# Sliding-window attention into a gated MLP on one core: batch 0's first eight groups lose their normalising pass, and the opening's list is put in another order

## The chip, the cores and the metric

The kernel runs on one core of one Trainium2 chip. The time is device microseconds (us) of one execution. The median of the runs before the change is 303.38 us (three runs, 303.17 to 303.96). The core has five engines that run side by side, each through its own instructions in order: TensorE (PE, matmuls; its weight loads are PEld), VectorE (DVE), ScalarE (ACT), GpSimd (POOL, which here also issues most loads) and SyncE (SP, which issues DMAs only). They wait for each other through semaphores. SBUF is the working memory, PSUM the memory that TensorE writes.

## What is computed

q, k and v are 8 batches x 8 heads x 576 positions x 64, in float32. A position attends to itself and the 63 before it:

```python
scores = (q @ k.T) / 8
mask = (rel >= 0) & (rel < 64)            # rel = pos_query - pos_key
scores = np.where(mask, scores, -1e9)
attn = np.exp(scores - scores.max(-1))
attn = attn / (attn.sum(-1) + 1e-9)
x = (attn @ v)                            # -> 4608 tokens x 512 (8 heads x 64)
h = x @ w_in                              # 512 x 2048
out = (h * np.cos(h)) @ w_out             # 2048 x 512 -> 4608 x 512, float32
```

## The kernel before

**Tiling.** The 4608 tokens are nine blocks of 512 (`mt`). Attention is worked in units of 64 queries by 128 keys (its own 64 keys and the 64 before). Two heads form a pair and share a unit: one head on partitions 0 to 63, the other on 64 to 127. A *group* is four units, so one 128x512 tile. The first eight groups (`n < n_first`) are batch 0: pair p, g = 0 for tokens 0 to 255 and g = 1 for tokens 256 to 511. The other groups are those of the later batches and of batch 0's last 64 tokens. Groups 8 to 18 are listed by hand too.

**One group, before.** `g_scores` (L296) writes the mask into PSUM by a matmul with the identity (L307) and adds the scores (L314). `g_max` (L320) takes the negated row maximum on DVE (L324). `g_exp` (L335) makes four exponentials on ACT, 128x128 each, with the row sum as a second result (L341, which the profile shows as ACTIVATE and ACTIVATION_READ_ACCUMULATOR). `g_inv` (L345) takes the reciprocal of the 128x4 sums on DVE (L351). `g_norm` (L354) multiplies the 128x512 exponentials by it, on POOL for the first eight groups (L358), and makes bfloat16 weights. `g_trans` (L367) transposes them on PE (L374), or by a DMA on SP's queue (L377) for groups not in `direct`; `g_put` (L380) copies the transposed weights to SBUF (through `copy`, L124). Every line 124 in the profile is that helper.

**Values and the first block.** `values_half(a, g)` (L405) multiplies the weights of pairs 2a and 2a+1 with v, for 256 tokens (L411); `put_x_half` (L415) copies the product to `xT` (L418, by L124). Block 0 goes in halves of 256 tokens: `first_half(g, f)` (L420) makes eight matmuls of 128x256 (L425) into one of five PSUM banks, `sine_half` (L429) takes the sine on ACT (L431), `gate_half` (L433) multiplies on DVE (L437) and frees the bank. A half of the block needs `xT` of both values of a. `second_part` (L439) is the second product (L444). Block 1 and later use lines 461, 692, 695 and 709.

**What sets the order.** The opening, up to the start of block 1, is one hand-written string, `FIRST` (L46 to L64). Each word is a step, recorded in that order on all engines: `Lq`, `Lk`, `Lv`, `Lwi`, `Lwo` are loads (POOL's queue, except pair 0's q and k of batch 0 by SP); `tq`/`tk` transposes and `pq`/`pk` their copies (capitals are batch 1); `s m e i n w c` the steps of a group named pair.g; `v` and `x` the values and their copy, named a.g; `h S g` first product, sine and gate, named half.f; `o` the second product; `zA zB zC` spread batch 0's v by 64 partitions; `tb` and `tb2` load ACT's tables; `G` words are groups 8 to 18. An engine thus does its share of the words from left to right. Each load of POOL's queue waits for the landing of the one eight before it. After the list, each block calls `pump`, which issues planned steps by their due times (`at`).

The small PSUM tiles with the tag "t" (transposes, values) come from a pool of three; the tiles "s" and "e" in SBUF from six.

Of the kernel before, what the change touches and what calls it, by code (L numbers as in the profile page):

```python
# [10 lines left out]
def _safe_warn(msg, *a, **kw):  # L11
# [3 lines left out]
F32 = mybir.dt.float32  # L15
BF16 = mybir.dt.bfloat16
AF = mybir.ActivationFunctionType
ALU = mybir.AluOpType
# [7 lines left out]
GF = 4  # L26
# [7 lines left out]
T = 2 * Q  # L34
LAGS = (0.2, 1, 3, 3.2, 3.8)
SKEW = 3
DIRECT = (0, 7, 8)
OUTS = 3
FILL = (6, 12)
TURNED = {4: 2, 5: 2, 6: 2, 7: 6}  # L40
# [3 lines left out]


FIRST = (  # L46
# [18 lines left out]
)  # L65


# [1 line left out]
def kernel(  # L69
# [9 lines left out]
    nc = tc.nc  # L79
    B, H, S, D = q.shape  # L80
    assert (B, H, S, D) == (8, 8, 576, 64)
    scale = 1.0 / math.sqrt(D)
# [8 lines left out]
    const = ctx.enter_context(tc.tile_pool(name="const", bufs=1))  # L91
    ld = ctx.enter_context(tc.tile_pool(name="ld", bufs=2))
    att = ctx.enter_context(tc.tile_pool(name="att", bufs=3))
    moe = ctx.enter_context(tc.tile_pool(name="moe", bufs=2))
    ps = ctx.enter_context(tc.tile_pool(name="ps", bufs=1, space=PSUM))
    ps_t = ctx.enter_context(tc.tile_pool(name="ps_t", bufs=3, space=PSUM))
# [9 lines left out]
    mask16 = const.tile([128, 6, 128], BF16, name="mask16")  # L106

    small = const.tile([128, 1], F32, name="small")
    w_sums = const.tile([128, 2, n_ff // 2, MT // 2], BF16, name="w_sums")

    st = {}
# [6 lines left out]
    half = MT // 2  # L118
# [4 lines left out]
    def copy(engine, out, in_):  # L123
        {"a": nc.scalar.copy, "p": nc.gpsimd.tensor_copy}.get(engine, nc.vector.tensor_copy)(out, in_)  # L124
# [126 lines left out]
    n_first = len(groups)  # L251
# [18 lines left out]
    last = n_listed + 4, n_listed + 5  # L270
    direct = set(range(n_first)) | {n_first + i for i in DIRECT} | set(last)

# [61 lines left out]

    def g_exp(n):  # L335
        s, negm = st.pop(("s", n)), st.pop(("m", n))
        e = att.tile([128, GF, 128], F32, tag="e", name="e", bufs=6)
        den = att.tile([128, GF], F32, tag="den", name="den", bufs=8)
        for u, (_, _, j, *_) in enumerate(groups[n]):
            c = slice(0, 128 if j or n < n_first else 64)  # L340
            nc.scalar.activation(e[:, u, c], s[:, u, c], AF.Exp, bias=negm[:, u:u + 1], scale=1.0 if n < n_first else -1.0,  # L341
                                 accum_out=den[:, u:u + 1])
        st["e", n] = e, den

    def g_inv(n):  # L345
        e, den = st["e", n]
        for u, (_, _, j, *_) in enumerate(groups[n]):
            if j == 0 and n >= n_first:
                nc.vector.memset(e[:, u, 64:128], 0.0)
        rden = att.tile([128, GF], F32, tag="rden", name="rden", bufs=8)  # L350
        nc.vector.reciprocal(out=rden[:, 0:len(groups[n])], in_=den[:, 0:len(groups[n])])  # L351
        st["r", n] = rden

    def g_norm(n, engine="p"):  # L354
        (e, _), rden = st.pop(("e", n)), st.pop(("r", n))
        w = att.tile([128, GF, 128], BF16, tag="w", name="w", bufs=8)
        u = len(groups[n])
        (nc.gpsimd if engine == "p" else nc.vector).tensor_tensor(out=w[:, 0:u], in0=e[:, 0:u], op=ALU.mult,  # L358
                                in1=rden[:, 0:u].unsqueeze(2).to_broadcast([128, u, 128]))
        st["w", n] = w  # L360

    def put_wT(n, wT):
        for i, (b, p, j, *h) in enumerate(groups[n]):
            for e in range(2):
                st["wT", (b, 2 * p + e, j, h[0]) if h else (b, p, j, e)] = wT[:, i, 64 * e:64 * e + 64]

    def g_trans(n):  # L367
        w, u = st.pop(("w", n)), len(groups[n])
        if n in direct:
            st["tw", n] = t_ps = ps_t.tile([128, GF, 128], BF16, tag="t", name="tw_ps")  # L370
            for i in range(GF if n == FILL[0] else 0):
                nc.tensor.transpose(t_ps[:, i], ident, ident)
            for i in range(u):
                nc.tensor.transpose(t_ps[:, i], w[:, i], ident)  # L374
            return
        wT = att.tile([128, GF, 128], BF16, tag="wT", name="wT", bufs=20)
        nc.sync.dma_start(out=wT[:, 0:u], in_=w[:, 0:u].rearrange("p u c -> p (u c)"), transpose=True)  # L377
        put_wT(n, wT)

    def g_put(n, engine=None):  # L380
        wT, u = att.tile([128, GF, 128], BF16, tag="wT", name="wT", bufs=20), len(groups[n])
        copy(engine, wT[:, 0:u], st.pop(("tw", n))[:, 0:u])
        put_wT(n, wT)


# [26 lines left out]
                                     lhsT=vtiles[0][:, max(j - 1, 0), 128 * (2 * a + p) + 64 * h:128 * (2 * a + p) + 64 * h + 64],  # L412
                                     rhs=st["wT", (0, 2 * a + p, j, h)], start=True, stop=True, skip_group_check=True)

    def put_x_half(a, g, engine=None):  # L415
        if ("xT", 0) not in st:
            st["xT", 0] = att.tile([128, PAIRS, MT], BF16, tag="xT", name="xT", bufs=2)
        copy(engine, st["xT", 0][:, 2 * a:2 * a + 2, half * g:half * g + half], st.pop(("o", a, g)))  # L418

    def first_half(g, f, which):  # L420
        st["h", g, f] = h_ps = bank(BANKS[which], "h_ps")
# [30 lines left out]
    def exp_table():  # L452
        nc.scalar.activation(small, small, AF.Exp, scale=0.0)
# [126 lines left out]
    for i, (b, jobs, banks) in enumerate(bursts):  # L580
        t = T * (b - 1)
# [49 lines left out]
    for n in range(16):  # L631
        i, f = divmod(n, 4)
# [6 lines left out]
        at(T + 4 - 0.1 * i, g_trans, n_listed - i)  # L639

    make_identity(nc, ident)
    nc.vector.memset(small, 0.0)
    exp_table()

    def spread_first(lo, hi):
# [15 lines left out]
             "y": lambda half_, engine: spread_v(1, half_, engine),  # L661
             "s": lambda p, g, which: g_scores(2 * p + g, which), "m": lambda p, g: g_max(2 * p + g),
             "e": lambda p, g: g_exp(2 * p + g), "i": lambda p, g: g_inv(2 * p + g),
             "n": lambda p, g, engine: g_norm(2 * p + g, engine), "w": lambda p, g: g_trans(2 * p + g),
             "c": lambda p, g, engine: g_put(2 * p + g, engine), "v": values_half, "x": put_x_half,
             "tb": sine_table, "tb2": exp_table, "h": first_half, "S": sine_half, "g": gate_half,
             "Gs": g_scores, "Gm": g_max, "Ge": g_exp, "Gi": g_inv, "Gn": g_norm, "Gw": g_trans, "Gc": g_trans,
             "Gp": g_put, "V": lambda p: values(1, p), "X": lambda p, engine: put_x(1, p, engine),
             "o": second_part, "oc": put_out}
    for step in FIRST.split():  # L670
# [5 lines left out]
    for mt in range(1, n_mt):  # L676
# [5 lines left out]
        for ff in range(n_ff):  # L682
# [8 lines left out]
            e = ff % 2  # L691
# [8 lines left out]
        for ms0 in range(0, MT // 128, 2):  # L700
            o_sb = moe.tile([128, 2, d_model], F32, tag="out", name="out_sb", bufs=OUTS)
            o_ps = [bank(which, "out_ps") for which in (("O1",) if mt == n_mt - 1 and ms0 else ("O1", "O0"))]
            for e in range(2):
# [4 lines left out]
                for ff in range(n_ff):  # L708
                    nc.tensor.matmul(out=o_ps[e], lhsT=gT[ff // 2][:, ff % 2, ms * 128:ms * 128 + 128],  # L709
                                     rhs=w_out_sb[:, ff], start=ff == 0, stop=ff == n_ff - 1)  # L710
# [38 lines left out]
```

## Time and profile before

| | |
|---|---|
| median of three runs | 303.38 us (303.17 to 303.96) |
| the profiled execution | 304.26 us, of which the span is 302.5 us |
| granted TensorE clock | 1.00 |
| PE busy | 290.5 us, 96% of the span |
| DVE busy | 233.8 us, 77% |
| ACT busy | 232.2 us, 77% |
| POOL busy | 208.7 us, 69% |
| first product of block 0 starts | 22.20 us after the span's start |
| its second product starts | 38.65 us |
| block 1's first product starts | 58.05 us |

In the profile's rows a line names the engine, the line of the kernel, the operation, the tile written and the tiles read, the shapes, and after "x" how many. A group row gives the busy time in us and the mean ns of one. A row of the timeline begins with the start and the length in us; the bracket is idle time of the engine just before it and what ended that time.

### The profile page before, as it was taken

Reading aid. Unit: us, or ns where it says so; the run is one execution under the profiler, and the core shown is the slowest. Engines: PE = TensorE matmul, PEld = TensorE weight load, DVE = VectorE, ACT = ScalarE, POOL = GpSimd, SP = SyncE. Lnnn points to the kernel's source line nnn. Section 1 sums busy time; section 2 is a strip of 40 time slices with the busy share of each in tenths; the row PEclk is TensorE's granted clock in tenths of the full one; section 3 lists DMA queues with packets and bytes.
Section 4 is the critical chain, followed back from the end, with each engine's and each line's share of the span. In section 5 each row is a group of like instructions: output and inputs, shape, how many; then the busy total and the mean of one; then the engine's idle time right before and its main releaser. Section 6 shows DMA issues by size and latency. Waiting matters only on the chain.

```text
span 302.5 us, 8484 instructions
## 1 busy us (share of the span) xinstructions
PE 290.5 (96%) x2920; PEld 162.4 (54%) x2920; DVE 233.8 (77%) x913; ACT 232.2 (77%) x781; POOL 208.7 (69%) x238
## 2 busy tenths in 40 slices
PE   3889999999999999999999999999999999999995
PEld 2668844554454544545454445444544454785484
DVE  3898877988887886788668875887688658985893
ACT  5898698877987699869986999689978997305610
POOL 7899558996799779987999699878995860000000
PEclk9999999999999999999999999999999999999999
DMA  7999999999999994999999998999599944003013
GB/s 150 180 205 168 196 192 133 102 136 155 237 125 111 219 158 88 98 143 185 198 105 155 164 183 118 136 196 178 110 110 128 198 84 156 0 3 141 1 35 106
DMA packets 158588, 41.47 MB, mean 137 GB/s; under 512 B 146960, under 2 KB 154192, under 8 KB 158544
## 3 DMA queue, kind: packets, MB, share of 16 engines
q0 software_dynamic: 100192, 18.06, 83.8%
q1 hardware_dynamic: 58352, 22.85, 41.5%
q8 instruction: 23, 0.38, 0.5%
q14 instruction: 21, 0.17, 0.2%
HBM read 36.70 MB, written 9.44 MB: 153 GB/s over the span
## 4 chain that ended last, share of the span: by engine, by line
PE 84%; DMA 11%; POOL 3%; DVE 1%; issue 1%; POOLq 0%
PE h_ps L461 37%; PE out_ps L709 28%; PE out_ps L555 8%; DMA w_out<-in_moe_w_out_dram 7%; DMA q<-in_q_dram 4%; PE out_ps L444 3%; PE s_ps L292 3%; PE o_ps L393 3%; POOL w L358 2%; PE tq_ps L206 1%; PE tw_ps L374 0%; DVE xT L124 0%; PE s_ps L314 0%; POOL w_in L191 0%; DVE negm L324 0%
## 5 line engine op out<-in xcount | busy, mean ns | idle before, releaser
L461 PE MATMUL h_ps<-xT,w_in 128*128 128x512 bf16 x512 | 115.1, 379 | 0.2
L695 DVE TENSOR_TENSOR gT<-h_ps,sin 128x512 bf16<-128x512 f32 x128 | 85.1, 688 | 25.8 <-ACT sin L692 25.2
L692 ACT ACTIVATE sin<-h_ps 128x512 f32<-128x512 f32 x128 | 73.8, 598 | 37.0 <-PE h_ps L461 36.7
L341 ACT ACTIVATE e<-s,negm 128x128 f32<-128x128 f32 (+1 forms) x256 | 97.1, 381 | 2.9 <-DVE negm L329 1.9
L709 PE MATMUL out_ps<-w_out,gT 128*128 128x512 bf16 x384 | 85.3, 379 | 0.0
L358 POOL TENSOR_TENSOR w<-e,rden 128x512 bf16<-128x512 f32 (+1 forms) x68 | 69.0, 1031 | 19.3 <-DVE rden L351 14.8
L461 PEld LDWEIGHTS <-w_in 128*128 128x128 bf16 x512 | 49.0, 98 | 54.5
L709 PEld LDWEIGHTS <-gT 128*128 128x128 bf16 x384 | 36.5, 98 | 43.1
L329 DVE CUSTOM_DVE_ANT_0 s<-s_ps,mask 128x128 f32<-128x128 f32 (+1 forms) x256 | 56.0, 277 | 2.5 <-PE s_ps L314 2.2
L341 ACT ACTIVATION_READ_ACCUMULATOR e<-s,negm 128x1 f32 x256 | 47.9, 187 | 0.0
L169 POOL DMA_DIRECT2D q<-in_q_dram x36 | 28.6, 796 | 9.7 <-DMA q<-in_q_dram 3.2
L175 POOL DMA_DIRECT2D v<-in_v_dram x40 | 34.2, 869 | 0.8 <-DMA q<-in_q_dram 0.6
L169 POOL DMA_DIRECT2D k<-in_k_dram x36 | 28.5, 794 | 2.4 <-DVE negm L329 0.9
L351 DVE RECIPROCAL rden<-den 128x4 f32<-128x4 f32 (+1 forms) x73 | 12.1, 166 | 18.3 <-ACT e L341 18.1
L124 POOL COPY v<-v 64x1536 bf16<-64x1536 bf16 (+3 forms) x16 | 22.9, 1431 | 0.4
L329 DVE DVE_READ_ACCUMULATOR2_ANT negm<- 128x1 f32 x256 | 21.3, 83 | 0.0
L124 DVE CAST xT<-o_ps 128x512 bf16<-128x512 f32 x24 | 15.5, 679 | 4.6 <-PE o_ps L393 4.4
L444 PE MATMUL out_ps<-w_out,gT 128*128 128x512 bf16 x64 | 15.0, 379 | 1.0 <-DMA w_out<-in_moe_w_out_dram 1.0
L425 PE MATMUL h_ps<-xT,w_in 128*128 128x256 bf16 x128 | 14.6, 273 | 0.0
L555 PEld LDWEIGHTS <-sums 128*128 128x128 bf16 x128 | 12.1, 98 | 2.0 <-DVE sums L504 0.4
L425 PEld LDWEIGHTS <-w_in 128*128 128x128 bf16 x128 | 12.3, 98 | 1.4
L124 ACT CAST xT<-o_ps 128x512 bf16<-128x512 f32 x12 | 7.1, 590 | 6.7 <-PE o_ps L393 6.4
(85 smaller groups left out, 307.8 us busy)
## 6 DMA issues: line engine op xcount, KB each, us to landing
out_dram<-out_sb SPq DMA_DIRECT2D x16, 512.0 KB, 7.5
v<-in_v_dram POOLq DMA_DIRECT2D x32, 128.0 KB, 5.9
q<-in_q_dram POOLq DMA_DIRECT2D x36, 96.0 KB, 8.5
k<-in_k_dram POOLq DMA_DIRECT2D x36, 96.0 KB, 8.5
w_in<-in_moe_w_in_dram POOLq DMA_DIRECT2D x4, 512.0 KB, 9.4
w_out<-in_moe_w_out_dram POOLq DMA_DIRECT2D x4, 512.0 KB, 11.7
q<-in_q_dram POOLq DMA_DIRECT2D x7, 144.0 KB, 6.5
k<-in_k_dram POOLq DMA_DIRECT2D x7, 144.0 KB, 6.5
```

What stands on the lines that cost most here:

```text
L124: {"a": nc.scalar.copy, "p": nc.gpsimd.tensor_copy}.get(engine, nc.vector.tensor_copy)(out, in_)
L169: nc.gpsimd.dma_start(out=st[name, b][:, c].rearrange("p (h d) -> p h d", h=H), in_=src.rearrange("h p d -> p h d"))
L175: nc.gpsimd.dma_start(out=vt.rearrange("p (h d) -> p h d", h=H), in_=v[b, :, c * 128:c * 128 + n, :].rearrange("h p d -> p h d"))
L329: nc.vector.tensor_tensor_reduce(out=s[:, u, c], in0=s_ps[:, u, c], in1=mask[:, 2 - j % 2 if j else 0, c], scale=-scale if b else -1.0, sc ...
L341: nc.scalar.activation(e[:, u, c], s[:, u, c], AF.Exp, bias=negm[:, u:u + 1], scale=1.0 if n < n_first else -1.0, accum_out=den[:, u:u + 1])
L358: (nc.gpsimd if engine == "p" else nc.vector).tensor_tensor(out=w[:, 0:u], in0=e[:, 0:u], op=ALU.mult, in1=rden[:, 0:u].unsqueeze(2).to_br ...
L425: nc.tensor.matmul(out=h_ps[:, half * e:half * e + half], lhsT=w_in_sb[:, ks, ff * 128:ff * 128 + 128], rhs=st["xT", 0][:, ks, half * g:ha ...
L461: nc.tensor.matmul(out=st["h", ff], lhsT=w_in_sb[:, ks, ff * 128:ff * 128 + 128], rhs=st["xT", mt][:, ks], start=start, stop=stop)
L555: nc.tensor.matmul(out=to[:, e] if type(to) is not list else to[e], lhsT=lhs[name][f // 2][:, f % 2, 128 * e:128 * e + 128], rhs=rhs[name] ...
L692: nc.scalar.activation(sin, h_ps, AF.Sin, bias=math.pi / 2.0)
L695: nc.vector.tensor_tensor(out=gt[:, e], in0=h_ps, in1=sin, op=ALU.mult)
L709: nc.tensor.matmul(out=o_ps[e], lhsT=gT[ff // 2][:, ff % 2, ms * 128:ms * 128 + 128], rhs=w_out_sb[:, ff], start=ff == 0, stop=ff == n_ff - 1)
```

## The change

1. For the first eight groups `g_exp` writes bfloat16 weights straight away (tile `w`), without the row sum; `g_inv` and `g_norm` are no longer called for them.
2. `sums_half` sums the transposed weights over the keys by matmuls with a 128x64 tile of ones, so that each of the 64 partitions of a head has the sum: four matmuls of 256 columns for a half of two pairs, 16 in all. `inv_half` takes the reciprocal of that 128x512 PSUM tile on DVE, and `put_x_half` multiplies the values with it on DVE instead of copying them.
3. The string `FIRST` has another order. The loads begin with the third pair (`Lk0.3`, `Lq0.2`); pair 1 comes last of batch 0's four. `zA`, `zB` and `zC` go to POOL.
4. `DIRECT` gets 3 and 6: groups 11 and 14 are transposed on PE and not by DMA.

```diff
-DIRECT = (0, 7, 8)
+DIRECT = (0, 3, 6, 7, 8)
...
 FIRST = (
...
+    "io mk Lk0.3 Lq0.2 Lk0.0 Lq0.0 Lk0.2 cq.d mc ck.a tk.0 tq.0 tk.3 pq.0.d pk.0.a tq.2 pq.2.d Lq0.3 s.0.0.4 tk.2 "
+    "s.0.1.3 Lk0.1 m.0.1 Lq0.1 Lk1.0 tq.3 Lq1.1 Lq1.0 pk.2.a Lv0.1 s.2.0.0 e.0.1 Lk1.1 Lv0.3 Lv0.0 m.0.0 pk.3.d "
+    "Lv0.2 pq.3.d tk.1 pk.1.a e.0.0 m.2.0 Lwi.0 Lwi.1 zA.0.p s.3.1.3 tq.1 s.3.0.4 Tk.0 w.0.0 pq.1.d zC.p e.2.0 "
+    "zA.1.p Lwi.2 m.3.0 s.1.1.1 Tq.1 Lk1.3 Lwi.3 c.0.0.a Pq.1.a Pk.0.a s.1.0.0 w.0.1 s.2.1.2 Tk.1 Tq.0 e.3.0 "
+    "m.1.1 m.1.0 c.0.1.d m.2.1 Pq.0.d Pk.1.a e.1.0 zB.1.p zB.0.p w.3.0 w.2.0 w.1.0 m.3.1 c.2.0.d c.3.0.d c.1.0.d "
+    "D.1.0 r.1.0 Lk1.2 Gs.9.4 v.1.0 x.1.0 e.3.1 e.1.1 v.0.0 D.0.0 r.0.0 Gs.12.1 Gs.10.0 Lv1.2 Lq1.3 w.1.1 w.3.1 "
+    "e.2.1 x.0.0 tb Gm.9 Gm.10 w.2.1 Gs.11.3 c.1.1.d h.0.0.2 h.0.1.0 D.0.1 Gm.12 c.3.1.d Gm.11 Lv1.1 Lwo.0 Lq1.2 "
+    "Lwo.1 S.0.1 g.0.1 S.0.0 c.2.1.a h.0.2.4 h.0.3.3 v.0.1 D.1.1 r.0.1 g.0.0 r.1.1 v.1.1 x.1.1 x.0.1 S.0.3 S.0.2 "
+    "h.0.5.0 g.0.3 h.0.4.2 Lv1.0 Lwo.2 h.1.0.1 Lq2.3 h.1.1.3 Tk.3 S.0.5 g.0.5 g.0.2 h.1.4.4 Lv1.3 S.1.0 S.1.1 "
+    "g.1.1 S.0.4 S.1.4 Pk.3.a g.0.4 g.1.0 g.1.4 h.0.6.0 h.1.5.3 h.1.6.1 Tk.2 Tq.3 S.0.6 S.1.5 h.1.3.4 h.0.7.2 "
...
+    ones = const.tile([128, 64], BF16, name="ones")
...
 def g_exp(n):
     s, negm = st.pop(("s", n)), st.pop(("m", n))
+    if n < n_first:
+        st["w", n] = w = att.tile([128, GF, 128], BF16, tag="w", name="w", bufs=8)
+        for u in range(GF):
+            nc.scalar.activation(w[:, u], s[:, u], AF.Exp, bias=negm[:, u:u + 1])
+        return
...
 def g_put(n, engine=None):
...
+    st["group", n] = wT
...
-def put_x_half(a, g, engine=None):
+def sums_half(a, g):
+    st["den", a, g] = d_ps = ps_t.tile([128, 2, half], F32, tag="t", name="d_ps")
+    for p in (0, 1):
+        for h in range(2):
+            d = slice(64 * h, 64 * h + 64)
+            nc.tensor.matmul(out=d_ps[d, p].rearrange("p (u c) -> p u c", c=64), lhsT=ones, rhs=st["group", 2 * (2 * a + p) + g][:, :, d],
+                             start=True, stop=True, skip_group_check=True)
+
+def inv_half(a, g):
+    st["inv", a, g] = inv = att.tile([128, GF, 128], F32, tag="s", name="inv", bufs=6)
+    nc.vector.reciprocal(out=inv.rearrange("p u c -> p (u c)"), in_=st.pop(("den", a, g)).rearrange("p a t -> p (a t)"))
+
+def put_x_half(a, g):
...
-    copy(engine, st["xT", 0][:, 2 * a:2 * a + 2, half * g:half * g + half], st.pop(("o", a, g)))
+    inv = st.pop(("inv", a, g)).rearrange("p u c -> p (u c)").rearrange("p (a t) -> p a t", a=2)
+    nc.vector.tensor_tensor(out=st["xT", 0][:, 2 * a:2 * a + 2, half * g:half * g + half], in0=st.pop(("o", a, g)), in1=inv,
+                            op=ALU.mult)
...
+nc.gpsimd.memset(ones, 1.0)
```

In the new list `D.a.g` is `sums_half`, `r.a.g` is `inv_half` and `x.a.g` the product into `xT`.

More of the change, by code (lines that the diff above doesn't have):

```diff
@@ L339, in g_exp @@
         for u, (_, _, j, *_) in enumerate(groups[n]):
-            c = slice(0, 128 if j or n < n_first else 64)
-            nc.scalar.activation(e[:, u, c], s[:, u, c], AF.Exp, bias=negm[:, u:u + 1], scale=1.0 if n < n_first else -1.0,
+            c = slice(0, 128 if j else 64)
+            nc.scalar.activation(e[:, u, c], s[:, u, c], AF.Exp, bias=negm[:, u:u + 1], scale=-1.0,
                                  accum_out=den[:, u:u + 1])
@@ L347, in g_inv @@
         for u, (_, _, j, *_) in enumerate(groups[n]):
-            if j == 0 and n >= n_first:
+            if j == 0:
                 nc.vector.memset(e[:, u, 64:128], 0.0)
@@ L664 @@
              "n": lambda p, g, engine: g_norm(2 * p + g, engine), "w": lambda p, g: g_trans(2 * p + g),
-             "c": lambda p, g, engine: g_put(2 * p + g, engine), "v": values_half, "x": put_x_half,
+             "c": lambda p, g, engine: g_put(2 * p + g, engine), "v": values_half, "D": sums_half, "r": inv_half, "x": put_x_half,
              "tb": sine_table, "tb2": exp_table, "h": first_half, "S": sine_half, "g": gate_half,
```

26 rows, old and new, of the table FIRST are left out of this document.

## The prediction

> **What bounds the kernel now.** I read the page's parts 1, 2 and 4 first (who is full, where, and what ended last), then the chain of waits in order of time, the timeline of PE, and the groups by form of DVE.
>
> ```profile
> PE 290.5 (96%) x2920; PEld 162.4 (54%) x2920; DVE 233.8 (77%) x913; ACT 232.2 (77%) x781; POOL 208.7 (69%) x238
> ...
> PE 84%; DMA 11%; POOL 3%; DVE 1%; issue 1%; POOLq 0%
> ```
>
> PE is full and makes 84% of the chain. Only what makes PE wait, or gives it more work, moves the end. Where PE waits is the beginning, so I cut the opening into stretches (width, then busy time of each engine):
>
> ```profile
> 0.00:22.20 22.20, 14.60 (x385) 11.46 (x386) 15.51 (x46) 17.31 (x70) 18.67 (x32) 1.00 1.25 177
> 22.20:38.65 16.45, 16.45 (x227) 14.33 (x223) 13.79 (x41) 13.13 (x29) 12.00 (x16) 1.00 1.17 185
> 38.65:58.05 19.40, 18.44 (x214) 9.67 (x210) 15.17 (x78) 16.71 (x78) 15.28 (x18) 1.00 1.59 143
> 58.05:90.01 31.96, 31.93 (x297) 16.00 (x296) 27.50 (x122) 27.29 (x100) 27.43 (x33) 1.00 2.02 162
> ```
>
> From 22.20 on PE is busy, but for 0.96 us in the third stretch; from 58.05 on nothing is lost. So a us later at the first product, or a us of PE idle before 58.05, is a us at the end. Up to 22.20 this is the chain (start, length, what), and the rows of PE that mark the stretches:
>
> ```profile
> 1.75 5.30 DMA q<-in_q_dram
> ...
> 7.33 6.82 DMA q<-in_q_dram
> ...
> 15.24 4.09 POOL w L358 x4
> ...
> 19.38 0.40 PE tw_ps L374 x4
> ```
> ```profile
> 7.17 0.74 PE L203 MATMUL tq_ps<-ident,q 64*64 64x64 bf16 x18
> 7.87 0.69 PE L203 MATMUL tk_ps<-ident,k 64*64 64x64 bf16 x18
> 8.37 0.62 PE L307 MATMUL s_ps<-mask,ident 64*64 64x512 bf16 x2
> 8.78 0.64 PE L314 MATMUL s_ps<-kT,qT 64*64 64x128 bf16 x8
> 9.21 0.69 PE L203 MATMUL tq_ps<-ident,q 64*64 64x64 bf16 x18
> ...
> 22.20 1.91 PE L425 MATMUL h_ps<-xT,w_in 128*128 128x256 bf16 x16
> ...
> 27.09 10.65 PE L425 MATMUL h_ps<-xT,w_in 128*128 128x256 bf16 x96
> 37.67 0.47 PE L203 MATMUL tk_ps<-ident,k 64*64 64x64 bf16 x18
> 37.98 0.73 PE L203 MATMUL tq_ps<-ident,q 64*64 64x64 bf16 x36
> 38.65 1.90 PE L444 MATMUL out_ps<-w_out,gT 128*128 128x512 bf16 x8
> ...
> 45.64 2.75 PE L444 MATMUL out_ps<-w_out,gT 128*128 128x512 bf16 x12 [0.61 <-DMA w_out<-in_moe_w_out_dram]
> ```
>
> POOL's normalising stands on the chain for 4.09 us, behind a load of w_in that had waited for the landing at 7.33 + 6.82 = 14.15. That is what the change removes. The question is what it puts in its place, and on which engine.
>
> **The change, part by part.** The new operation without a row is the reciprocal of a 128x512 PSUM tile, four times. Before has it only for 128x4 and 128x3. The rows near it:
>
> ```profile
> L695 DVE TENSOR_TENSOR gT<-h_ps,sin 128x512 bf16<-128x512 f32 x128 | 85.1, 688 | 25.8 <-ACT sin L692 25.2
> ...
> L329 DVE CUSTOM_DVE_ANT_0 s<-s_ps,mask 128x128 f32<-128x128 f32 x228 | 52.5, 284 | 1.2 <-PE s_ps L314 0.9 <-PE s_ps L292 0.3
> ...
> L351 DVE RECIPROCAL rden<-den 128x4 f32<-128x4 f32 x69 | 11.5, 166 | 18.3 <-ACT e L341 18.1
> ...
> L329 DVE CUSTOM_DVE_ANT_0 s<-s_ps,mask 128x64 f32<-128x64 f32 x28 | 5.2, 217 | 1.3 <-PE s_ps L314 1.3
> ...
> L528 DVE TENSOR_TENSOR out_sb<-out_ps,t 128x256 f32<-128x256 f32 x4 | 1.6, 422 | 0.7 <-PE out_ps L555 0.6
> ...
> L351 DVE RECIPROCAL rden<-den 128x3 f32<-128x3 f32 x4 | 0.7, 168 | 0.0
> ```
> ```profile
> L351 DVE RECIPROCAL rden<-den x73: 115/177/180, 13.7 to 246.0; 128x4 f32<-128x4 f32 x69, 128x3 f32<-128x3 f32 x4
> ```
> ```profile
> 43.03 0.12 DVE L351 RECIPROCAL rden<-den 128x4 f32<-128x4 f32 x1
> 43.07 0.19 DVE L329 CUSTOM_DVE_ANT_0 s<-s_ps,mask 128x64 f32<-128x64 f32 x1
> ```
>
> An ordinary DVE operation costs (688 - 422)/256 = 1.04 ns an element and 688 - 533 = 155 ns besides; by L329's two forms 1.05 and 150. Lower bound: the reciprocal is ordinary, 0.69 us. For it speaks that three elements take no less than four. Upper bound: the operation behind one starts 0.04 us later, so an element takes at most 10 ns, 512 x 10 + 155 = 5.3 us. Between them: the median of the reciprocals, 177 ns for four elements, is 22 to 27 ns above 155 and 150, where four ordinary elements are 4. That is 5.5 to 6.75 ns an element, 3.0 to 3.6 us for 512. I take 3.3 us, the middle; by the mean of 166 instead it would be 2.75 to 4 ns, 1.6 to 2.2 us.
>
> The Trainium skill's page "VectorE: DVE Perf Modes", section "First, the fixed hardware budget", says that a reciprocal runs as an iterative divide with a repeat count of 8. As an estimate from that page, at its 0.96 GHz, an element would be 8.3 ns and the tile 4.3 us plus the fixed part, which is the first rival below; the trace agrees that an element costs more than an ordinary one, and puts it lower.
>
> *Up to the first reciprocal.* Rows of DVE and ACT that give the pace:
>
> ```profile
> 9.46 0.69 DVE L324 TENSOR_REDUCE negm<-s_ps 128x4 f32<-128x512 f32 x1
> 10.06 0.75 DVE L227 TENSOR_SCALAR qT<-tq_ps 128x576 bf16<-128x576 bf16 x1
> ...
> 12.44 0.75 DVE L124 COPY kT<-tk_ps 128x576 bf16<-128x576 bf16 x1
> 13.11 0.68 DVE L324 TENSOR_REDUCE negm<-s_ps 128x4 f32<-128x512 f32 x1
> ```
> ```profile
> 20.05 0.39 DVE L124 COPY wT<-tw_ps 128x512 bf16<-128x512 bf16 x1
> 20.36 0.28 DVE L329 CUSTOM_DVE_ANT_0 s<-s_ps,mask 128x128 f32<-128x128 f32 x1
> 20.57 0.08 DVE L329 DVE_READ_ACCUMULATOR2_ANT negm<- 128x1 f32 x1
> ```
> ```profile
> 8.49 0.36 ACT L341 ACTIVATE e<-s_ps,negm 128x128 f32<-128x128 f32 x1
> 8.74 0.20 ACT L341 ACTIVATION_READ_ACCUMULATOR e<-s_ps,negm 128x1 f32 x1
> 8.83 0.37 ACT L341 ACTIVATE e<-s_ps,negm 128x128 f32<-128x128 f32 x1
> ```
>
> A reduction holds DVE 0.60 us, a 576-wide copy 0.67, a copy of weights 0.31, one masked tile 0.21. The new list puts two more transposes and a second group's scores ahead of the first reduction: the second load of POOL's queue lands near 7.05 + 0.9 = 7.9 (the first lands at 1.75 + 5.30, the ninth at 14.15), then two transposes (0.50 each, as from 7.87 to 8.37) and two groups of scores (0.84, from 8.37 to 9.21) take 2.7 us, so it starts near 10.6. Behind it, up to the first reciprocal, DVE has 8 x 0.60 + 4 x 0.67 + 4 x 0.31 = 8.7 us, which would end at 19.3. ACT has five groups of exponentials (1.0 us each without the sum's read-out, which takes 0.09 of the 0.34 a tile) and five copies, taken at 0.67 too: 8.35 us from 11.3, then a transposition (0.40), a copy (0.39) and four sums (0.11 each at most, like the 256-wide product): 20.9. The later one sets it; I take 21.0. The first product began at 22.20 in before, so POOL's 4.09 us are not won: DVE and ACT, and pair 1 coming last, are late next.
>
> *From there to the first product.* Two reciprocals and two products of the kind of L695, all on DVE, nothing beside them that PE could use: 2 x 3.3 + 2 x 0.65 = 7.9. The first product starts at 28.9, 6.7 us later than 22.20.
>
> *The other half of the tokens.* From 28.9 DVE has 14 masked tiles of groups 9 to 12 (2.9), two copies (0.6), two gates (1.2, L695's kind), two reciprocals (6.6), two products (1.3): 12.6, to 41.5. PE gets through six of the sixteen blocks of first product in that time and waits for the rest, since the second half of xT comes last. Then ten blocks of 8 x 0.111 = 0.89 and four transposes of 0.32 are left, 10.2 us (0.111 is 10.65/96): the second product starts at 51.7, against 38.65, 13.1 later. The sixteen sums, 1.8 us of PE at most, stand in the time in which PE waits for DVE.
>
> *Second product.* PE was busy 18.44 of 19.40. Its 0.96 of idle time, of which the wait for w_out at 45.64 is 0.61, goes: w_out's last quarter came at 45.64 and is wanted after 55 here, and one load of batch 2 that now stands ahead of it (`Lq2.3`) takes about 0.9 of these nine. One of batch 1's transposes (`Tk.3`, 0.32) has moved ahead of it, and groups 11 and 14 add seven transposes (0.4; 0.40 for four in the row at 19.38, overlapping). So 18.5: 0.9 won back. I add 0.2 for xT of block 1, whose copies wait for these two groups. Afterwards nothing changes. Sum: +13.1 - 0.9 + 0.2 = +12.4 us.
>
> *At nothing:* POOL's eight products of 1.04 leave, and it waits for nothing they did. But three of its five copies of v now stand ahead of w_in's third quarter, on a queue where each load waits for the eighth before it: some 3.1 us later at the pace of its passes (4.09/4). In before no first product waited for w_in, and the first product is 6.7 us later, so at least 3.6 us cover this; without cover it would count in full. SP loses three spreads of v and two DMA transposes, which nothing waits for here. ACT's 32 reads, 0.09 each, are in the sum.
>
> PE's clock: 18 transposes at 7.87 took 0.69 us against 0.47 at 37.67, so before shows a slow state at the start, and none later. PE would now idle some 3 us beside each reciprocal; I add nothing for it. The Trainium skill's page "TensorE: Matmul & The Clock Gate", Part 1, says that PE falls to half its clock after an idle window of about 3.4 us and needs as long a busy one to come back; as an estimate from that page, one lapse after the second half of xT would add 1.7 us. No row of before can show it.
>
> **Rivals.** (1) DVE passes each element of a reciprocal eight times: 8 x 1.04 = 8.3 ns, 4.4 us; four times 1.1 more, +16.8: 320.2 us. For it: it lies under the bound of 10 ns; against it: the 33 ns that it puts on four elements exceed the 27. This is the rule of the Trainium skill's page "VectorE: DVE Perf Modes" given above. (2) The reciprocal is ordinary, 0.69 us. The first product starts at 21.0 + 2.7 = 23.7, PE is then full as before (16.45 us), the second product starts at 40.2, 1.5 late, less 0.7: 304.2. For it: three elements as slow as four. (3) Faster: with (2), the chain's 4.09 us come off after all, if ACT and DVE are fed early, so that the first reciprocal starts at 16.9 instead of 21.0: 300.1. With that start the sign turns where four reciprocals cost 12.4 - 4.1 = 8.3 us less than 4 x 3.3, at 1.2 us each. Against it: the two ledgers above, which already reach 19.3 and 20.9. (4) No difference: DVE's work hides beside PE's. Against it: the first product needs both values of xT.
>
> **How the numbers follow.** The profiled execution took 304.26 us, 0.88 above the median of 303.38; its span is 302.5. The shift of 12.4 goes on the median: 315.8 us. Chances: forecast 0.68; (1) 0.15; (2) 0.08; (3) 0.04; (4) 0.02; other delays 0.03. The range: 2.2 us a reciprocal gives 4.4 less, 311.4; 4.4 us gives 320.2, and the upper bound of 5.3 us 323.8; I stop at 311 and 321.5, which leaves out (2), (3), (4) and the highest part of the bound, 0.17 in all. A change under 0.3% (0.9 us) can't be told from none. (3) and a little of (2) make faster 0.05; most of (2) would lie within 0.3%, so with (4) same is 0.06; slower 0.89.
>
> **What would show it.** The 128x512 reciprocals near 3.3 us each in the groups by form; the first product near 29, the second near 52, block 1 near 70; PE's idle time in the opening ended by xT and gates of DVE. No waits for w_out. Wrong: reciprocals of 0.7 us, a first reciprocal before 18, or a wait for w_in.

## The result, and the profile after

The changed kernel takes 321.0 us (median of four runs, 320.7 to 321.4) where the kernel before takes 303.56 us beside it (four runs, 303.17 to 303.96): a ratio on record of 1.0585, 95% interval 1.0562 to 1.0607 (the two medians alone give 1.0575). The kernel before is now and then one or two per cent slower without a change; two such runs (307.65 and 308.98 us, beside the last three experiments) are left out below. The profiled execution took 320.7 us, with a span of 318.9 us. The forecast was 315.8 us: the direction and most of the amount are there, and 5.2 us more.

The page of the changed kernel: busy time, the clock that TensorE was granted in 40 slices of the span, and the chain that ended last, by engine.

```profile
PE 296.4 (93%) x2912; PEld 165.4 (52%) x2943; DVE 248.5 (78%) x912; ACT 229.5 (72%) x750; POOL 201.4 (63%) x232
...
PEclk9995979999999999999999999999999999999999
...
PE 82%; DVE 7%; ACT 4%; DMA 3%; issue 1%; POOL 1%; POOLq 0%; SPq 0%; DVEq 0%
```

PE's share falls from 96% to 93%, DVE makes 7% of the chain in place of 1%, and the clock, which was 9 in all slices before, shows a 5 and a 7. The stretches of the opening, cut where first product, second product and block 1 begin (start:end, width, busy time of PE, PEld, DVE, ACT and POOL, then granted clock, DMA share, GB/s):

```profile
0.00:29.22 29.22, 17.86 (x401) 12.86 (x402) 21.50 (x40) 17.04 (x47) 22.69 (x40) 0.90 1.28 181
29.22:54.75 25.53, 21.00 (x243) 16.05 (x241) 19.40 (x39) 10.26 (x19) 7.09 (x9) 0.85 1.07 124
54.75:73.89 19.14, 18.83 (x200) 9.65 (x200) 17.14 (x83) 16.95 (x78) 10.85 (x13) 1.00 0.50 48
73.89:318.90 245.01, 238.67 (x2076) 126.83 (x2103) 190.50 (x753) 185.24 (x608) 160.77 (x171) 1.00 1.17 129
```

Against the widths of before (22.20, 16.45, 19.40, and 302.5 - 58.05 = 244.45) that is +7.02, +9.08, -0.26 and +0.56: 16.40 us of span, 16.1 of it ahead of the second product. (The medians differ by 17.4: the profiled execution of before, 304.26 us, lies 0.70 above its median, and that of after 0.30 below.) DVE's rows of the two new kinds, grouped by form over the run, and then as they stand in the opening's timeline:

```profile
L432 DVE RECIPROCAL inv<-d_ps 128x512 f32<-128x512 f32 x4 | 13.4, 3352 | 0.0
```
```profile
19.97 3.36 DVE L432 RECIPROCAL inv<-d_ps 128x512 f32<-128x512 f32 x1
23.44 0.69 DVE L438 TENSOR_TENSOR xT<-o_ps,inv 128x512 bf16<-128x512 f32 x1
24.06 3.36 DVE L432 RECIPROCAL inv<-d_ps 128x512 f32<-128x512 f32 x1
27.45 0.69 DVE L438 TENSOR_TENSOR xT<-o_ps,inv 128x512 bf16<-128x512 f32 x1
33.48 0.69 DVE L458 TENSOR_TENSOR gT<-h_ps,sin 128x512 bf16<-128x512 f32 x1 [1.86 <-ACT sin L452]
34.09 3.35 DVE L432 RECIPROCAL inv<-d_ps 128x512 f32<-128x512 f32 x1
37.36 0.63 DVE L458 TENSOR_TENSOR gT<-h_ps,sin 128x512 bf16<-128x512 f32 x1
37.90 3.35 DVE L432 RECIPROCAL inv<-d_ps 128x512 f32<-128x512 f32 x1
41.35 1.29 DVE L438 TENSOR_TENSOR xT<-o_ps,inv 128x512 bf16<-128x512 f32 x2
```

Four reciprocals of 3.35 us, two of them ahead of the first product and two ahead of the other half. But DVE also stood still for 1.86 us before the third one, for a sine. PE's timeline shows why:

```profile
23.38 0.64 PE L427 MATMUL d_ps<-wT,ones 128*64 128x256 bf16 x4 [2.39 <-DVE inv L432]
...
29.22 3.60 PE L446 MATMUL h_ps<-xT,w_in 128*128 128x256 bf16 x16
...
33.32 1.96 PE L446 MATMUL h_ps<-xT,w_in 128*128 128x256 bf16 x16
...
42.69 2.67 PE L446 MATMUL h_ps<-xT,w_in 128*128 128x256 bf16 x16 [2.90 <-DVE xT L438]
...
50.75 3.67 PE L446 MATMUL h_ps<-xT,w_in 128*128 128x256 bf16 x32
```

The same sixteen matmuls take 1.96 us at 33.32 and 3.60 us at 29.22: the first blocks ran at half clock, so their sines came late, and DVE, with the third reciprocal in its queue behind the gate that needs that sine, waited. After x of the other half (42.64) sixteen take 2.67 us. So there are two candidates, the reciprocals themselves and the clock that PE lost while it waited for them, beside the new order of the list.

### The profile page after: what moved, and what is told of

It is laid out like the page before. It is cut to its first block, busy times and chain, and to the rows that moved or that the text cites. A ratio compares the mean times of both kernels' runs of the same rounds, so it can differ in the third digit from the quotient of the medians.

```text
span 318.9 us, 8428 instructions
## 1 busy us (share of the span) xinstructions
PE 296.4 (93%) x2912; PEld 165.4 (52%) x2943; DVE 248.5 (78%) x912; ACT 229.5 (72%) x750; POOL 201.4 (63%) x232
## 4 chain that ended last, share of the span: by engine, by line
PE 82%; DVE 7%; ACT 4%; DMA 3%; issue 1%; POOL 1%; POOLq 0%; SPq 0%; DVEq 0%
PE h_ps L482 35%; PE out_ps L731 22%; PE out_ps L576 8%; PE out_ps L465 4%; PE h_ps L446 4%; DVE inv L432 4%; PE o_ps L400 2%; PE s_ps L293 2%; DMA wT<-w 2%; ACT e L347 2%; DMA q<-in_q_dram 1%; PE tq_ps L207 1%; PE tw_ps L380 1%; PE s_ps L315 1%; ACT w L341 1%
## 5 line engine op out<-in xcount | busy, mean ns | idle before, releaser
L717 DVE TENSOR_TENSOR gT<-h_ps,sin 128x512 bf16<-128x512 f32 x128 | 85.0, 688 | 24.7 <-ACT sin L714 24.0
L714 ACT ACTIVATE sin<-h_ps 128x512 f32<-128x512 f32 x128 | 73.8, 598 | 37.1 <-PE h_ps L482 35.3
L364 POOL TENSOR_TENSOR w<-e,rden 128x512 bf16<-128x512 f32 (+1 forms) x57 | 58.5, 1043 | 42.9 <-DVE rden L357 40.7
L731 PE MATMUL out_ps<-w_out,gT 128*128 128x512 bf16 x372 | 82.9, 379 | 1.7 <-issue 1.6
L482 PEld LDWEIGHTS <-w_in 128*128 128x128 bf16 x512 | 48.8, 98 | 54.5 <-issue 0.4
L125 POOL COPY v<-v 64x512 bf16<-64x512 bf16 (+3 forms) x20 | 25.8, 1290 | 2.6 <-DMA v<-in_v_dram 2.1
L357 DVE RECIPROCAL rden<-den 128x4 f32<-128x4 f32 (+1 forms) x65 | 10.8, 167 | 18.1 <-ACT e L347 17.8
L452 ACT ACTIVATE sin<-h_ps 128x512 f32<-128x512 f32 x16 | 9.0, 598 | 19.9 <-PE h_ps L446 19.8
L446 PE MATMUL h_ps<-xT,w_in 128*128 128x256 bf16 x128 | 18.0, 306 | 2.9 <-DVE xT L438 2.9
L446 PEld LDWEIGHTS <-w_in 128*128 128x128 bf16 x128 | 13.5, 109 | 6.4 <-issue 3.3
L465 PE MATMUL out_ps<-w_out,gT 128*128 128x512 bf16 x61 | 15.0, 380 | 0.2
L458 DVE TENSOR_TENSOR gT<-h_ps,sin 128x512 bf16<-128x512 f32 x16 | 10.3, 681 | 6.0 <-ACT sin L452 6.0
```

Of the source, the lines that this page charges most:

```text
L446: nc.tensor.matmul(out=h_ps[:, half * e:half * e + half], lhsT=w_in_sb[:, ks, ff * 128:ff * 128 + 128], rhs=st["xT", 0][:, ks, half * g:ha ...
L465: nc.tensor.matmul(out=st["out", m], lhsT=st["g", ff // 2][:, ff % 2, m * 128:m * 128 + 128], rhs=w_out_sb[:, ff], start=ff == 0, stop=ff ...
L482: nc.tensor.matmul(out=st["h", ff], lhsT=w_in_sb[:, ks, ff * 128:ff * 128 + 128], rhs=st["xT", mt][:, ks], start=start, stop=stop)
L714: nc.scalar.activation(sin, h_ps, AF.Sin, bias=math.pi / 2.0)
L717: nc.vector.tensor_tensor(out=gt[:, e], in0=h_ps, in1=sin, op=ALU.mult)
```

## The experiments

Theory A: the loss is the four reciprocals on DVE, plus half clock on PE after its waits for them. Rival B: the new list with its moved loads costs by itself. Rival C: the slow clock is hidden behind DVE. All times below stand beside runs of the kernel before: 303.99 us for the first four, 303.32 us for the last three, where the changed kernel had 303.56. A few tenths of a us between two experiments are therefore not resolved.

**1. An ordinary operation in place of the reciprocal.**

```diff
-        nc.vector.reciprocal(out=inv..., in_=d_ps...)
+        nc.vector.tensor_scalar(inv..., d_ps..., 1 / 512, None, ALU.mult)
```

> The changed kernel with each 128x512 reciprocal replaced by a multiplication of the same tile by a constant, so the division by the sums is left out; list, matmuls and products stay. Theory A (the reciprocals' length and the slow clock of PE that their waits bring make the loss): the four operations take about 0.69 us each in place of 3.35. The first product starts at 29.22 - 2 x 2.66 = 23.9 or a little before, PE is then full for 16.5 as in the kernel before, the second product starts near 40.4 and block 1 near 59.5, against 58.05 before: 305 us, 303.5 to 306. The granted clock shows no stretch near 0.5 after the start. Rival B (the new list, with its moved loads and pair 1 coming late, costs by itself): 309 us or more, with the second product after 44. Rival C (only DVE's time counts, the clock does not): 321.0 - 4 x 2.66 = 310.4.

Measured: 306.69 us (306.58 to 307.66), ratio 1.0109, 95% interval 1.0074 to 1.0143. The operation's group by form, and then the stretches of this kernel:

```profile
L432 DVE TENSOR_SCALAR inv<-d_ps 128x512 f32<-128x512 f32 x4 | 2.8, 689 | 0.3 <-PE d_ps L427 0.2
```
```profile
0.00:23.60 23.60, 16.14 (x401) 11.85 (x401) 15.85 (x36) 16.84 (x46) 19.71 (x36) 1.00 1.24 174
23.60:41.01 17.41, 17.33 (x244) 14.38 (x241) 14.43 (x43) 10.46 (x20) 10.06 (x14) 1.00 1.48 196
41.01:59.93 18.92, 18.92 (x204) 9.55 (x199) 16.92 (x81) 16.74 (x78) 10.62 (x13) 1.00 1.11 97
```

14.3 of the 17.4 us go with four operations that are 4 x 2.66 = 10.7 us shorter, more than their length; the clock is whole (1.00 in all three stretches). Rival C in its strict form (310.4) falls, rival B (309 or more) too. The time is 0.7 us above the upper end of what theory A gave, since the second stretch lasts 17.41 us and not 16.5.

**2. The reciprocals stay, PE is kept busy in its four waits.**

```diff
+    def keep_busy(which, n):
+        f_ps = bank(BANKS[which], "f_ps")
+        for i in range(n):
+            nc.tensor.matmul(out=f_ps, lhsT=ident, rhs=mask16[:, 0:4]..., start=True, stop=True, skip_group_check=True)
 FIRST:  ... v.0.0 +F.0.9 D.0.0 ... w.1.1 +F.3.5 w.3.1 ... r.1.1 +F.1.6 v.1.1 ... Lwo.2 +F.1.11 h.1.0.1 ...
```

> The changed kernel with 31 further 128x512 matmuls on unused PSUM tiles, whose results nobody reads, in the four gaps in which PE waits for a reciprocal: 9 before the sums of half 0 of pairs 0 and 1, 5 before the transposition of the last group of pair 3, 6 before the values of pairs 2 and 3, 11 before the first block of the other half. At some 0.22 us each they fill 2.0, 1.1, 1.3 and 2.4 us of gaps of 2.39, 1.59, 1.62 and 2.90. Theory A: PE stays at full clock, the windows from 24 to 50 us show 0.95 or more in place of 0.50, DVE no longer waits 1.86 us for a sine at 33.5, the second product starts near 51 in place of 54.75, and the time is 321.0 - 3.7 = 317.3 us, 316.5 to 318.5. Rival C (the slow clock is hidden behind DVE): the clock rises, but the time stays within 0.3% of 321.0. Rival D (the clock falls from something else than idle PE): the clock stays near 0.5, time 321 or more.

Measured: 317.10 us (316.98 to 317.49), ratio 1.0447, interval 1.0414 to 1.0480, clear of the changed kernel's 1.0562 to 1.0607. Its stretches:

```profile
0.00:28.87 28.87, 19.69 (x415) 13.66 (x415) 21.09 (x36) 17.04 (x47) 23.10 (x41) 1.00 1.29 183
28.87:51.33 22.46, 21.32 (x262) 15.96 (x258) 19.61 (x43) 10.26 (x19) 6.68 (x9) 1.00 1.22 142
51.33:70.25 18.92, 18.92 (x204) 9.54 (x199) 16.92 (x81) 16.74 (x78) 10.63 (x13) 1.00 0.48 47
70.25:315.70 245.45, 241.44 (x2109) 127.10 (x2104) 190.85 (x755) 185.56 (x608) 160.87 (x171) 1.00 1.16 129
```

More work on PE makes the kernel 3.9 us faster: the clock stays at 1.00 and the second product starts at 51.33 in place of 54.75. Rival C and rival D fall. What is left between this kernel and experiment 1 is 10.4 us, close to the 10.7 by which the reciprocals are longer.

**3 and 4. The old order.** Experiment 3 runs the new arithmetic in the list of before: the words for the normalising are taken out, sums and reciprocal are put directly before each product with the values, and `DIRECT` is the old one. Experiment 4 is the same with experiment 1's ordinary operation.

```diff
-DIRECT = (0, 3, 6, 7, 8)
+DIRECT = (0, 7, 8)
 FIRST of before, with
-  ... i.0.0 ... n.1.0.p ... x.0.0.a ... x.0.1.a x.1.1.d ...
+  ... D.0.0 r.0.0 x.0.0 ... D.0.1 r.0.1 x.0.1 D.1.1 r.1.1 x.1.1 ...
```

> The new arithmetic in the order of the kernel before: the steps for the normalising leave the old list, sums and reciprocals stand directly before each product with the values, the groups turned by TensorE for batch 1 are the old ones. Theory A: the four reciprocals of 3.35 us cost as much here, 319 to 325 us. Rival B (the new list is what costs): the time falls by most of the loss, to 311 us or less. If the new list was worth something, this is slower than 321.0 by up to 4 us.

> The old order of the run before with the multiplication by a constant in place of the reciprocal, so again without the division by the sums. With the other two it completes a table of two orders by two operations. Theory A: 303.5 to 306.5 us, within 1.5 us of the new order with the ordinary operation; the operation is worth 14 us or more in either order. Rival B: the old order with the ordinary operation is 4 us or more below the new order with it.

Measured: 322.96 us (321.49 to 323.99; ratio 1.0634, interval 1.0580 to 1.0688) with the reciprocal, 310.38 us (309.36 to 310.65; ratio 1.0217, interval 1.0181 to 1.0253) without it. So rival B falls in the other direction: the new list is worth 3.7 us with the ordinary operation. With the reciprocal the medians differ by 2.0 us, which is not clear of noise, since the two intervals overlap; the clock differs too, 0.75 in experiment 3 between first and second product where the changed kernel has 0.85. Two statements of theory A failed here: experiment 4 lies 3.7 us from experiment 1 and not within 1.5, and the operation is worth 12.6 us in the old order and not 14. PE's timeline of experiment 4:

```profile
24.57 0.38 PE L380 MATMUL tw_ps<-ident,w 128*128 128x128 bf16 x4 [1.56 <-DVE inv L432]
24.80 3.65 PE L446 MATMUL h_ps<-xT,w_in 128*128 128x256 bf16 x16
...
33.73 0.41 PE L427 MATMUL d_ps<-wT,ones 128*64 128x256 bf16 x4 [0.79 <-DVE inv L432]
...
36.38 8.89 PE L446 MATMUL h_ps<-xT,w_in 128*128 128x256 bf16 x80 [1.26 <-DVE gT L458]
```

In the old order the second half's sums (`D.1.1`) stand in PE's queue between the blocks and wait for a PSUM tile of the pool of three that the operation before must free; the blocks behind them wait too, and DVE's gates behind the operations. And sixteen matmuls take 3.65 us here as well: even a wait of 1.56 us was followed by half clock.

**5. No division at all.** The four sums and the four operations are taken out, and the product with the values is one multiplication by a constant.

```diff
 FIRST:  -D.0.0 -D.0.1 -D.1.0 -D.1.1 -r.0.0 -r.0.1 -r.1.0 -r.1.1
-        nc.vector.tensor_tensor(out=xT..., in0=o_ps, in1=inv, op=ALU.mult)
+        nc.vector.tensor_scalar(xT..., o_ps, 1 / 128, None, ALU.mult)
```

> The changed kernel without the four sums by TensorE and without the four 128x512 operations that make their reciprocals; each product with the values becomes one multiplication by a constant of the same tile. The division by the sums is left out altogether. It shows what the whole idea could have won had its new work cost nothing. Theory A (DVE's and ACT's own work sets the first product, POOL's 4.09 us on the chain are covered): two operations of 0.69 leave the way to the first product, 23.60 - 1.4 = 22.2, as in the kernel before, and the time is within 1.2 us of the run before, 302.5 to 305. Rival F (POOL's pass was on the path in full): the first product starts near 18 to 20 and the time is 301 or less. Rival B (the list and the rest of the change cost something even so): 305.5 or more.

Measured: 305.89 us (305.12 to 308.08, seven runs), ratio 1.0095, interval 1.0063 to 1.0126: not faster than the kernel before, with less work. Rival F falls. Theory A's band (up to 305) is missed by 0.9 us, and the time lies in rival B's (305.5 or more): some 2.6 us by the medians, 1.1 us by the two profiled spans (303.6 and 302.5), belong to the rest of the change. The first two stretches, and what ACT, DVE and PE do ahead of the first product:

```profile
0.00:23.12 23.12, 15.17 (x393) 11.39 (x393) 15.37 (x42) 16.44 (x46) 19.76 (x37) 1.00 1.25 178
...
23.12:39.63 16.51, 16.51 (x236) 14.12 (x233) 12.41 (x33) 10.90 (x21) 10.02 (x13) 1.00 1.45 197
```
```profile
17.95 4.31 ACT L341 ACTIVATE w<-s_ps,negm 128x128 bf16<-128x128 f32 x16
...
20.17 1.46 DVE L437 TENSOR_SCALAR xT<-o_ps 128x512 bf16<-128x512 f32 x2 [0.27 <-PE o_ps L418]
...
21.27 0.38 PE L301 MATMUL s_ps<-mask,ident 128*128 128x512 bf16 x1 [0.38 <-ACT w L341]
...
22.03 0.84 PE L380 MATMUL tw_ps<-ident,w 128*128 128x128 bf16 x12
```

With POOL's pass gone and nothing in its place, the first product starts at 23.12, 0.92 later than before. Both products with the values are done at 21.63 (20.17 + 1.46). PE waits 0.38 us for ACT's exponentials, up to 21.27, and from there it has 1.85 us of scores and transposes of other groups ahead of the first product in its queue. So in this list the 4.09 us that POOL's pass had on the chain of before were not to be won; no run tests a list that puts the first product further ahead. The second stretch is 16.51 where experiment 1 has 17.41. Experiment 1 has eight more matmuls there (x244 against x236), the two sums of the second half, and PE is busy 0.82 us longer: about that is what these sums cost once PE is full.

**6 and 7. One lapse at a time.** A lapse is a time in which PE is granted half its clock; the changed kernel has two in its opening. Experiment 2 with only the first two groups of extra matmuls (9 and 5), and with only the last two (6 and 11).

```diff
 experiment 6, against experiment 2:  -F.1.6 -F.1.11
 experiment 7, against experiment 2:  -F.0.9 -F.3.5
```

> The changed kernel with only the first two of the four groups of unread matmuls (9 before the sums of pairs 0 and 1, 5 before the last transposition of pair 3), so that PE stays warm up to the first product and may cool down before the other half of the tokens. Theory A (each lapse costs by itself): the lapse from 24 to 32 us goes, x of the second half comes near 41.0 in place of 42.64, the lapse from 44 to 46 stays, and the time is 319.2 us, 318.5 to 319.8. Rival G (the first lapse is all that counts, since only its slow blocks are waited for): 317.1 as with all four. Rival H (only the second counts): 321.

> The changed kernel with only the last two groups of unread matmuls (6 before the values of pairs 2 and 3, 11 before the other half of the tokens). Theory A: the lapse from 24 to 32 us stays, with DVE's wait for a sine near 33.5; the one from 44 to 46 goes, and the time is 318.9 us, 318.3 to 319.6. Rival G: 321. Rival H: 317.1.

Measured: 319.51 us (319.04 to 319.92) with the first two, 318.97 us (317.54 to 319.97) with the last two; 317.10 with all four, 321.0 with none. Each lapse costs by itself: the first 1.5 us (321.0 - 319.5) to 1.9 (319.0 - 317.1), the second 2.0 (321.0 - 319.0) to 2.4 (319.5 - 317.1), together the 3.9. Both lie where theory A put them. The intervals are wide beside these steps: that of experiment 6 (1.0495 to 1.0565) still touches that of the changed kernel, and that of experiment 7 (1.0449 to 1.0545) overlaps that of experiment 2, so by themselves they exclude rival G but not rival H. The profiles speak against rival H: the second product starts at 53.24 and 53.21, each 1.5 us sooner than with no filling (54.75) and 1.9 us later than with both (51.33).

The nine kernels side by side (us; medians, the rest from the profiled execution):

| kernel | first product | second product | block 1 | span | median |
|---|---|---|---|---|---|
| before | 22.20 | 38.65 | 58.05 | 302.5 | 303.56 |
| after | 29.22 | 54.75 | 73.89 | 318.9 | 321.0 |
| 1 ordinary operation | 23.60 | 41.01 | 59.93 | 304.8 | 306.7 |
| 2 PE kept busy | 28.87 | 51.33 | 70.25 | 315.7 | 317.1 |
| 3 old order | 29.52 | 58.40 | 76.64 | 321.1 | 323.0 |
| 4 old order, ordinary operation | 24.80 | 46.18 | 64.41 | 308.9 | 310.4 |
| 5 no division | 23.12 | 39.63 | 58.55 | 303.6 | 305.9 |
| 6 first lapse filled | 29.21 | 53.24 | 72.16 | 317.4 | 319.5 |
| 7 second lapse filled | 29.50 | 53.21 | 72.13 | 318.2 | 319.0 |

None of these beats the kernel before, and since experiment 5 leaves out all the work that divides and is still not faster, no cheaper reciprocal in this list is likely to.

## Why the prediction was right in most terms, and where it failed

- **The reciprocal's length: right.** 3.3 us was taken from what four elements cost beyond the fixed part; it is 3.352 us, (3352 - 155)/512 = 6.24 ns an element. The Trainium skill's page "VectorE: DVE Perf Modes", section "First, the fixed hardware budget", gives a reciprocal a repeat count of 8; the estimate made from it was 8.3 ns an element. The measurement decides: 6.24 ns, six times the 1.04 ns of an ordinary element. Rival (1), which rested on eight, gave 320.2 us and so came nearer to 321.0 than the forecast, by a mechanism that the row refutes. Its number was close only because of the term that I had left out.
- **The range, 311 to 321.5, holds 321.0: luck in part.** Its upper part was there for a reciprocal of more than 3.3 us; nothing in it stood for the clock, whose 3.9 us took the time up there.
- **First reciprocal at 21.0: it started at 19.97.** The ledger of DVE and ACT was 1.0 us too long.
- **First product at 28.9: 29.22, by two errors that cancel.** The way from the first reciprocal to it took 9.25 us and not 7.9 (8.83 at full clock, from 20.04 to 28.87 in experiment 2). The reciprocals and products were priced right (19.97 to 28.14 for both pairs), but behind the second product PE still had transposes and the scores of group 11 in its queue ahead of the first block.
- **Second product at 51.7: 54.75.** With PE kept warm it is 51.33. The working of this stretch (12.6 us of DVE, then ten blocks) held; the speed of PE within it did not.
- **"I add nothing for it": this is the step that failed.** Of PE's clock I wrote that before shows a slow state at the start only, and put the term at zero although I had PE idle some 3 us beside each reciprocal. It is worth 3.9 us by experiment 2. The rule of the Trainium skill's page "TensorE: Matmul & The Clock Gate", Part 1, was the right warning. The 1.7 us estimated from it were for one lapse after the second half of xT; that lapse cost 2.0 to 2.4 us, and the one that I did not see, from 23.19 to 33.44, lasted 10.2 us and cost 1.5 to 1.9.
- **Second stretch of products, -0.9 + 0.2: right.** 18.92 us in experiments 1, 2, 5, 6 and 7 and 19.14 after, where I had 18.7; none of its matmuls waits for w_out.
- **The sums at nothing: right where PE waits for DVE.** With the shorter operation PE is full, the cover is gone, and the two sums of the second half cost about 0.82 us (experiment 1 against experiment 5). Rival (2), 304.2 us for an ordinary operation, is too low, 306.7, in part for that.
- **POOL's 4.09 us not won: right,** by experiment 5, for this list. Rival (3) falls: with an ordinary operation the kernel takes 306.7 us and not 300.1, and the operation starts at 19.87 and not 16.9.
- **Nothing later: nearly.** The forecast and the 3.9 us make 319.7; 1.3 us remain by the medians. In the two profiles the span grows by 16.40 us, within 0.1 of 12.4 + 3.9, so most of the rest is the distance of the profiled executions from their medians. Behind block 1's start the kernels with the new list take 244.9 to 246.1 us against 244.45, those with the old list 244.46 and 244.49 (from the table). What these 0.4 to 1.6 us are stays open; no run took them apart.

## What to carry to other kernels

Price a long operation on one engine twice: by its own length, and by what the engine that waits for it loses in clock afterwards. Before moving a pass away from the engine that the chain names, add up the work of the other engines up to the same point; if that work ends no earlier, moving the pass wins nothing, as here. A reciprocal belongs on the smallest tile: 128x4, the sums of one group, costs 0.17 us; the sums of two groups spread over 128x512 cost 3.35.

## What the runs showed of the hardware

In these runs the clock does not fall after a wait of a certain length; it steps on a grid. Where the granted clock changes within the changed kernel's opening, the edges lie at 23.19, 33.44, 43.68 and 47.08, so 10.25, 10.24 and 3.40 us apart: three, three and one steps of 3.41. In experiment 6 the lapse runs from 41.01 to 44.43, in experiment 7 from 22.11 to 32.35, so again one step and three, but at other places of the span. Cut along that grid (start:end, width, PE busy, clock, DMA share, GB/s):

```profile
19.77:23.19 3.42, 1.22 (x44) 1.00 1.24 206
23.19:26.60 3.41, 2.50 (x21) 0.50 1.23 206
26.60:30.02 3.42, 2.41 (x20) 0.50 1.73 182
30.02:33.44 3.42, 3.42 (x19) 0.50 1.32 202
33.44:36.85 3.41, 2.43 (x36) 1.00 1.47 197
36.85:40.26 3.41, 2.29 (x32) 1.00 1.61 189
40.26:43.68 3.42, 0.99 (x10) 1.00 1.59 191
43.68:47.08 3.40, 3.40 (x33) 0.50 1.46 105
47.08:50.50 3.42, 3.42 (x56) 1.00 0.03 2
```

A step with 1.22 or 0.99 us of work sets the next one to half clock, although no single wait in it reached 3 us. At half clock a step with 2.4 or 2.5 us of work does not bring it back, a full one does; at full clock 2.3 to 2.4 us keep it in this kernel. That is why a wait of 2.39 us cost 10.2 us of half clock, and the longer one of 2.90 us only 3.4: behind the first PE was only partly busy, behind the second full. In experiment 4 (first two rows) a step with 1.66 us of work was enough, and one slow step followed; in experiment 7 (next two) the clock fell behind a step with 2.36; in experiment 6 (last three) it held behind one with 1.68 and fell behind one with 0.62:

```profile
21.78:25.19 3.41, 1.66 (x22) 1.00 1.21 240
25.19:28.61 3.42, 3.31 (x18) 0.50 1.23 204
```
```profile
18.70:22.11 3.41, 2.36 (x52) 1.00 1.24 204
22.11:25.52 3.41, 1.86 (x17) 0.50 1.23 207
```
```profile
34.19:37.60 3.41, 1.68 (x28) 1.00 1.51 193
37.60:41.01 3.41, 0.62 (x6) 1.00 1.65 189
41.01:44.43 3.42, 3.31 (x16) 0.50 1.63 189
```

So busy time alone gives no threshold: 1.68 us kept the clock in one kernel, 1.66 and 2.36 us lost it in two others. What else counts in such a step stays open; no run here tests it. The Trainium skill's page "TensorE: Matmul & The Clock Gate", Part 1, speaks of a free-running window of 3413 ns, and the trace agrees with that length and, by the different places of the grid in the spans, with its running free of the kernel's work. The page's idle window is no empty one here, by the steps above.
